# Windowed attention with a fused feed-forward: how many tokens of Q and K lie in one partition, and how the block transposes are cut

## The chip, the cores and the metric

One core of one Trainium2 chip. The metric is the device time of one execution in microseconds (us). The kernel before took 408.87 us, the median of two runs (408.53 and 409.21).

## The reference, cut to what matters

```python
# q, k, v: [8 batches, 8 heads, 576 tokens, 64], float32; window 64, causal
scores = q @ k.T / 8;  mask = (0 <= i - j) & (i - j < 64)
attn   = softmax(where(mask, scores, -1e9)) @ v
x      = attn.transpose(0, 2, 1, 3).reshape(4608, 512)
out    = ((x @ w1) * (x @ w2)) @ w3 @ w_out          # w1, w2: 512x1024, w3: 1024x1024, w_out: 1024x512
```

## The kernel before, in words

The order of the work on every engine is written out by hand; each engine runs its own queue in that order. There are three strands.

**Attention, batch by batch.** `load_qk` (L199) brings Q or K of one batch into a tile `t16` of 128 partitions, cast from float32 to float16 on the way, by two DMAs of GpSimd (POOL), L203. Each DMA takes four of the eight heads (`hh` is the head's parity). A head lies in 32 partitions, and a partition holds TI = 18 consecutive tokens of 64 values: one run of 4,608 bytes in DRAM and 2,304 bytes in the tile. `transposes` (L206) then has VectorE (DVE) transpose 32x32 blocks, one instruction for K or Q and one head parity (L211): it reads 32 values of one token at a time, and what it writes along a row of `kT` or `qT` are the tokens of 32 partitions, which lie 18 positions (36 bytes) apart. Four such instructions make one batch. The tiles `t16`, `kT` and `qT` have two buffers each. `load_v` (L217, L223) loads V by DMAs of POOL, a block of 128 tokens of all heads at a time (rows of 64 values: 256 bytes in DRAM, 128 in the tile).

`scores(n)` (L235, matmul L249) makes the scores of a third of a batch in two PSUM tiles `a_ps` (both buffers of that pool); `weigh` takes their exponential on ScalarE (ACT, L259) and masks it with two `affine_select` on POOL (L267, L269). `values(d)` (a half of that third) multiplies with V (matmuls L296 for the first two batches, L312 after), again into `a_ps`; ACT forms the reciprocal of the sums by Ln and Exp (L302, L303 or L318 to L320), and DVE multiplies it in and writes `xT` (L304, or L321 and L322).

**The feed-forward**, nine groups of 512 tokens. `ffn_ab` (matmul L374, 8 for one of eight feature blocks) makes a and b in PSUM tiles `f_ps` (four buffers), ACT copies a out (L379), DVE multiplies (L380). `ffn_o` (matmul L392) multiplies with the product of w3 and w_out; DVE copies the result out (L394) and the SP queue stores it.

**The fold** of w3 with w_out, at the start: eight steps of transposes on TensorE (PE, L430), a DVE copy (L432), matmuls (L438) and a copy (L439). The weights come by DMAs of POOL (L413, L417, L423).

Order: K and Q of batch 0 are loaded first, then w_out and half of w3, then V and the rest; four transposes; the scores of batch 0 between fold steps; K and Q of batch 1; the values of batch 0; then `ffn_ab` of group 0 with the four transposes of batch 1 and the scores of batch 1; then the values of batch 1 with the four transposes of batch 2; then a loop over twelve ticks for a batch (`tick`, L342 on) in which the feed-forward of groups 1 to 8 is laid between. In a tick `scores` comes at every fourth, `values` at the next two. The list `late` says what else: K of the batch two ahead is loaded in tick 0 of a batch, Q in tick 1; V of the next batch in ticks 2, 3 and 5; the transposes of the next batch stand in ticks 1, 3, 5 and 7. Every DMA that POOL issues reports on one of eight completion counters, handed out in turn, so each waits for the one eight places before it.

Of the kernel before, what the change touches and what calls it, by code (L numbers as in the profile page):

```python
# [144 lines left out]
def kernel(  # L145
# [11 lines left out]
    nc = tc.nc  # L157
    B, H, S, D = q.shape
# [4 lines left out]
    NJ = H // 2  # L163
    TI = 18
# [31 lines left out]

    t16s, kTs, qTs = {}, {}, {}

    def load_qk(b, which):  # L199
        src = k if which == "k" else q  # L200
        t = sb.tile([P, 2, TI * D], FP16, name=which + "16", bufs=2)
        for hh in range(2):
            nc.gpsimd.dma_start(out=t[:, hh], in_=src[b, hh:H:2].rearrange("j (p r) d -> j p (r d)", r=TI))  # L203
        t16s[which, b] = t

    def transposes(b, which, hh):  # L206

        dst = kTs if which == "k" else qTs
        if hh == 0:
            dst[b] = sb.tile([P, 2, 2, S], FP16, name=which + "T")  # L210
        nc.vector.transpose(dst[b][:, hh].rearrange("q c (p i) -> q i c p", i=TI), t16s[which, b][:, hh].rearrange(  # L211
            "p (i c e) -> p i c e", c=2, e=32))

    def v_heads(b):
        return v16s[b % 2].rearrange("p c j (a e) -> p c (j a) e", a=2)[:, :, :, 0:D]
# [118 lines left out]
    def event(b, kind, ahead, *a):  # L334
        if b + ahead >= B:
            return
        do = {"load": load_qk, "t": transposes, "v": load_v, "copy": copy_v}[kind]
        do(b + ahead, *a)
# [102 lines left out]
    rows = 2 * 3 * B  # L441
# [32 lines left out]
    def fold_step(fc):  # L474
        if fc + 1 < 8:
            w3Ts[fc + 1] = fold_t(fc + 1)
        fold_mm(fc, w3Ts.pop(fc), act_cp if fc % 4 == 3 else dve_cp)

    load_qk(0, "k")
    load_qk(0, "q")  # L480
    load_wo()
    load_w3(0)
# [3 lines left out]
    for hh in range(2):  # L486
        transposes(0, "k", hh)
        transposes(0, "q", hh)
# [140 lines left out]
```

## Time and profile before

| | us |
|---|---|
| median of the two runs | 408.87 |
| the profiled execution, its own time | 407.49 |
| its span in the profile | 405.8 |

The profiled execution is one further run; its time is 1.69 us longer than the span that the profile covers. Busy time of an engine is summed over its instructions. PEclk is the clock granted to TensorE as a share of its full 2.4 GHz; 0.50 is its lower level, 1.2 GHz. The DMA column is the mean busy share of 16 DMA engines (over 1 where packets overlap).

### The profile page before, as it was taken

What the parts mean: (1) busy time and instruction counts of PE and PEld (TensorE: products, weight loads), DVE (VectorE), ACT (ScalarE), POOL (GpSimd) and SP (SyncE); (2) the same over time, 40 slices, a digit from 0 to 9 for tenths busy, and PEclk for the clock granted to TensorE, in tenths of its full rate; (3) what the DMA queues carried; (4) which work ended last, traced back from release to release, by engine and by line L of the source; (5) the groups of instructions that cost most, each with busy time, mean ns of one, the idle gap of its engine ahead of it and who ended that gap; (6) DMA issues with size and microseconds to landing.
All of it is one profiled execution on the core that took longest, in us unless ns stands there. A gap on an engine that the chain in (4) does not pass through costs nothing.

```text
span 405.8 us, 6273 instructions
## 1 busy us (share of the span) xinstructions
PE 291.7 (72%) x2474; PEld 153.8 (38%) x2474; DVE 300.1 (74%) x267; ACT 149.7 (37%) x256; POOL 169.0 (42%) x218
## 2 busy tenths in 40 slices
PE   8008895747067454987679567978696779999995
PEld 8006452223033212443234233855342335455442
DVE  2892756976956399779977997598969896655542
ACT  1003162125023602364426433524464337764220
POOL 6307943118046852186127704535424533540300
PEclk9757999569668855996889887989899789999999
DMA  5990499911409990129312980299206410020203
GB/s 61 203 188 17 40 165 160 144 15 32 48 28 104 121 128 0 54 69 138 22 52 62 133 38 27 80 124 52 80 28 39 46 55 29 26 80 1 106 1 107
DMA packets 64097, 29.47 MB, mean 73 GB/s; under 512 B 51088, under 2 KB 54416, under 8 KB 64064
## 3 DMA queue, kind: packets, MB, share of 16 engines
q0 software_dynamic: 58640, 19.45, 51.3%
q1 hardware_dynamic: 5280, 9.46, 6.6%
q8 instruction: 20, 0.33, 0.4%
q14 instruction: 13, 0.11, 0.1%
q10 hardware_dynamic: 144, 0.13, 0.1%
HBM read 38.80 MB, written 9.44 MB: 119 GB/s over the span
## 4 chain that ended last, share of the span: by engine, by line
PE 40%; DVE 26%; issue 16%; DMA 10%; POOL 6%; ACT 1%; DVEq 0%; POOLq 0%
PE f_ps L374 22%; PE f_ps L392 11%; DVE qT L211 10%; DVE kT L211 9%; DMA k<-in_k_dram 7%; PE a_ps L312 4%; DMA q<-in_q_dram 3%; DVE ab L380 3%; PE a_ps L249 2%; POOL pt L269 2%; POOL pt L267 2%; DVE xT L322 2%; DVE xT L321 1%; DVE t2k L394 1%; POOL v L223 1%
## 5 line engine op out<-in xcount | busy, mean ns | idle before, releaser
L374 PE MATMUL f_ps<-xT,w_sb 128*128 128x512 f16 (+1 forms) x640 | 151.5, 392 | 30.1 <-DVE ab L380 23.8
L267 POOL TENSOR_SCALAR_AFFINE_SELECT pt<-pt 128x512 f16<-128x512 f16 (+1 forms) x64 | 52.0, 813 | 169.8 <-ACT pt L259 169.8
L374 PEld LDWEIGHTS <-w_sb 128*128 128x128 f16 x640 | 64.3, 104 | 99.3 <-issue 52.4
L211 DVE STREAM_TRANSPOSE kT<-k 128x1152 f16<-128x1152 f16 x16 | 81.9, 5119 | 16.4 <-DMA k<-in_k_dram 16.1
L259 ACT ACTIVATE pt<-a_ps 128x1024 f16<-128x1024 f32 (+1 forms) x48 | 43.1, 950 | 118.3 <-PE a_ps L249 118.3
L211 DVE STREAM_TRANSPOSE qT<-q 128x1152 f16<-128x1152 f16 x16 | 82.1, 5134 | 0.1
L392 PE MATMUL f_ps<-wc_sb,ab 128*128 128x512 f16 (+1 forms) x296 | 75.9, 411 | 7.6 <-DVE ab L380 7.6
L380 DVE TENSOR_TENSOR ab<-f_ps,a_sb 128x512 f16<-128x512 f32 x72 | 51.4, 723 | 32.9 <-PE f_ps L374 18.4
L379 ACT COPY a_sb<-f_ps 128x512 f32<-128x512 f32 x72 | 41.8, 581 | 62.6 <-PE f_ps L374 62.6
L249 PE MATMUL a_ps<-qT,kT 32*128 32x128 f16 (+1 forms) x768 | 19.2, 234 | 63.2 <-DVE xT L322 29.0
L269 POOL TENSOR_SCALAR_AFFINE_SELECT pt<-pt 128x512 f16<-128x512 f16 (+1 forms) x64 | 51.9, 811 | 4.4
L392 PEld LDWEIGHTS <-ab 128*128 128x128 f16 x296 | 29.7, 105 | 44.3 <-issue 10.3
L223 POOL DMA_DIRECT2D v<-in_v_dram x40 | 34.1, 856 | 19.5 <-DMA k<-in_k_dram 17.4
L249 PEld LDWEIGHTS <-kT 32*128 32x128 f16 x768 | 13.7, 103 | 74.4 <-issue 44.2
L394 DVE COPY t2k<-f_ps 128x512 f32<-128x512 f32 (+1 forms) x36 | 24.8, 693 | 13.1 <-PE f_ps L392 12.4
L321 DVE TENSOR_TENSOR xT<-a_ps,r 64x384 f16<-64x384 f32 x36 | 19.6, 546 | 19.0 <-ACT r L320 19.0
L318 ACT ACTIVATE ln_s<-a_ps 64x384 f32<-64x384 f32 x36 | 17.5, 487 | 40.1 <-PE a_ps L312 40.0
L312 PEld LDWEIGHTS <-v 128*128 128x128 f16 x288 | 20.4, 106 | 9.2 <-issue 3.2
L312 PE MATMUL a_ps<-pt,v 128*128 128x128 f16 (+1 forms) x288 | 23.0, 229 | 0.0
L322 DVE TENSOR_TENSOR xT<-a_ps,r 64x384 f16<-64x384 f32 x36 | 20.2, 561 | 0.5
L320 ACT ACTIVATE r<-ln_s 128x384 f32<-128x384 f32 x36 | 18.8, 523 | 1.1
L319 ACT ACTIVATE ln_s<-a_ps 64x384 f32<-64x384 f32 x36 | 17.4, 482 | 0.4
(41 smaller groups left out, 147.5 us busy)
## 6 DMA issues: line engine op xcount, KB each, us to landing
out_dram<-t2k SPq DMA_DIRECT2D x35, 256.0 KB
k<-in_k_dram POOLq DMA_DIRECT2D x16, 288.0 KB, 11.4
q<-in_q_dram POOLq DMA_DIRECT2D x16, 288.0 KB, 12.1
v<-in_v_dram POOLq DMA_DIRECT2D x32, 128.0 KB, 11.1
w_sb<-in_moe_w_dram POOLq DMA_DIRECT2D x4, 512.0 KB, 12.2
ab<-in_moe_w_out_dram POOLq DMA_DIRECT2D x1, 1024.0 KB, 15.7
ab<-in_moe_w_dram POOLq DMA_DIRECT2D x2, 512.0 KB, 18.2
xT<-in_moe_w_dram POOLq DMA_DIRECT2D x2, 512.0 KB, 14.7
```

The lines of the kernel that those rows point to most:

```text
L211: nc.vector.transpose(dst[b][:, hh].rearrange("q c (p i) -> q i c p", i=TI), t16s[which, b][:, hh].rearrange("p (i c e) -> p i c e", c=2, ...
L223: nc.gpsimd.dma_start(out=vh[lo:P, c], in_=v[b, :, s0:s0 + P - lo, :].rearrange("h s d -> s h d"))
L249: nc.tensor.matmul(s_ps[j // 2][:, j % 2, o0:o0 + m], kT[part, a, c, k0:k0 + P], qT[part, a, c, q0:q0 + m], start=(c == 0), stop=(c == 1), ...
L259: nc.scalar.activation(pt[:, :, :, 0:w], s_ps, AF.Exp, bias=-SHIFT, scale=scale)
L267: nc.gpsimd.affine_select(out=sl, in_=sl, pattern=pat, compare_op=ALU.is_ge, fill=0.0, base=off, channel_multiplier=-1)
L269: nc.gpsimd.affine_select(out=sl, in_=sl, pattern=[[-s, m] for s, m in pat], compare_op=ALU.is_ge, fill=0.0, base=63 - off, channel_multip ...
L312: nc.tensor.matmul(o_ps[:, jj, o0:o0 + n], v16[:, si * 2 + bi, j0 + jj, a * D:a * D + P], pt[:, jj, a, c0:c0 + n], start=first, stop=(bi = ...
L374: nc.tensor.matmul(d[:, f * n + c0:f * n + c1], w[:, dc, (fc + f) * P:(fc + f + 1) * P], xT[:, dc, xc:xc + c1 - c0], start=first, stop=(dc ...
L379: act_cp(a_sb[:, 0:nf * n], a_ps[:, 0:nf * n])
L380: nc.vector.tensor_tensor(ab[:, fc:fc + nf, lo:hi], b_ps[:, 0:nf * n].rearrange("p (f n) -> p f n", f=nf), a_sb[:, 0:nf * n].rearrange("p ...
L392: nc.tensor.matmul(o_ps[:, 0:c1 - c0], ab[:, fc, t * P:t * P + P], wc_sb[:, fc, c0:c1], start=(fc == 0), stop=(fc == 7))
L394: cp(o_sb[:, c0:c1], o_ps[:, 0:c1 - c0])
```

## The change

A partition now holds two consecutive tokens (r = 2) of each of nine runs: head token 64 i + 2 p + r' is in partition p, run i. The DMAs are cut by pairs of heads (`j`), four for a load in place of two, each to 32 partitions; a run is 512 bytes in DRAM and 256 in the tile, 18 for each partition and DMA. The transposes are issued for each half `c` of the head dimension (32 of the 64 values), so two instructions of 576 elements a partition stand where one of 1152 stood; the tokens that one writes along a row lie two positions (4 bytes) apart. Tiles, buffers, matmuls and the order of the calls stay as they are.

```diff
+    def run(b):
+
+        return 2
+
     def load_qk(b, which):
         src = k if which == "k" else q
+        r = run(b)
         t = sb.tile([P, 2, TI * D], FP16, name=which + "16", bufs=2)
-        for hh in range(2):
-            nc.gpsimd.dma_start(out=t[:, hh], in_=src[b, hh:H:2].rearrange("j (p r) d -> j p (r d)", r=TI))
+        for j in range(NJ):
+            nc.gpsimd.dma_start(
+                out=t[32 * j:32 * j + 32].rearrange("p hh (i n) -> p (hh i) n", n=r * D),
+                in_=src[b, 2 * j:2 * j + 2].rearrange("hh (i p r) d -> p (hh i) (r d)", p=32, r=r))
         t16s[which, b] = t
 
     def transposes(b, which, hh):
 
         dst = kTs if which == "k" else qTs
+        r = run(b)
         if hh == 0:
             dst[b] = sb.tile([P, 2, 2, S], FP16, name=which + "T")
-        nc.vector.transpose(dst[b][:, hh].rearrange("q c (p i) -> q i c p", i=TI), t16s[which, b][:, hh].rearrange(
-            "p (i c e) -> p i c e", c=2, e=32))
+        rows = t16s[which, b][:, hh].rearrange("p (i r d) -> p i r d", r=r, d=D)
+        for c in range(2):
+            nc.vector.transpose(dst[b][:, hh, c].rearrange("q (i p r) -> q i r p", p=32, r=r),
+                                rows[:, :, :, 32 * c:32 * c + 32])
```

## Rows read from the trace of the kernel before

**Rows 1.** The page's busy times, and the chain that ended last by engine.

```profile
PE 291.7 (72%) x2474; PEld 153.8 (38%) x2474; DVE 300.1 (74%) x267; ACT 149.7 (37%) x256; POOL 169.0 (42%) x218
PE 40%; DVE 26%; issue 16%; DMA 10%; POOL 6%; ACT 1%; DVEq 0%; POOLq 0%
```

**Rows 2.** The page's groups of instructions: the transposes, and two DVE groups beside them.

```profile
L211 DVE STREAM_TRANSPOSE kT<-k 128x1152 f16<-128x1152 f16 x16 | 81.9, 5119 | 16.4 <-DMA k<-in_k_dram 16.1
L211 DVE STREAM_TRANSPOSE qT<-q 128x1152 f16<-128x1152 f16 x16 | 82.1, 5134 | 0.1
L380 DVE TENSOR_TENSOR ab<-f_ps,a_sb 128x512 f16<-128x512 f32 x72 | 51.4, 723 | 32.9 <-PE f_ps L374 18.4
...
L432 DVE COPY t2k<-f_ps 128x1024 f16<-128x1024 f16 x8 | 5.3, 675 | 6.1 <-PE f_ps L430 6.1
```

**Rows 3.** Busy time by stage: stretch, length, engines, PEclk, DMA share, GB/s.

```profile
59.50:125.00 65.50, 33.86 (x290) 15.12 (x289) 50.78 (x29) 17.03 (x29) 23.30 (x30) 0.77 0.74 73
125.00:340.00 215.00, 160.56 (x1280) 82.06 (x1279) 178.75 (x160) 91.31 (x158) 97.45 (x124) 0.84 0.61 69
340.00:395.00 55.00, 55.00 (x393) 27.02 (x393) 30.22 (x49) 28.36 (x50) 16.40 (x19) 1.00 0.11 40
```

**Rows 4.** The same stretches, L211 alone: DVE busy (count), PEclk, DMA share, GB/s.

```profile
59.50:125.00 65.50, 40.75 (x8) 0.77 0.74 73
125.00:340.00 215.00, 102.39 (x20) 0.84 0.61 69
```

**Rows 5.** Timeline of DVE, then of PE, around 200 us: start, length, instruction.

```profile
192.66 5.12 DVE L211 STREAM_TRANSPOSE kT<-k 128x1152 f16<-128x1152 f16 x1
...
198.97 0.56 DVE L322 TENSOR_TENSOR xT<-a_ps,r 64x384 f16<-64x384 f32 x1
...
199.58 0.64 PE L249 MATMUL a_ps<-qT,kT 32*128 32x128 f16 x30 [3.64 <-DVE xT L322]
200.16 3.17 PE L392 MATMUL f_ps<-wc_sb,ab 128*128 128x512 f16 x7
```

**Rows 6.** The chain in order of time: start, length, what.

```profile
1.61 9.65 DMA k<-in_k_dram
11.29 5.10 DVE kT L211
...
26.23 4.93 DVE qT L211
...
304.15 0.46 PE a_ps L312 x8
...
348.48 0.56 PE a_ps L249 x32
...
379.90 12.09 PE f_ps L374 x56
```

**Rows 7.** Timeline of POOL, its DMA issues at the start and at 41 us.

```profile
1.61 1.63 POOL L203 DMA_DIRECT2D k<-in_k_dram  x2 [0.15 <-issue]
...
11.55 0.88 POOL L223 DMA_DIRECT2D v<-in_v_dram  x1 [3.76 <-DMA k<-in_k_dram]
...
41.45 1.59 POOL L223 DMA_DIRECT2D v<-in_v_dram  x2
```

**Rows 8.** Three stretches of one microsecond: PEclk, DMA share and GB/s end the line.

```profile
6.00:7.00 1.00, 1.00 (x22) 1.00 (x20) 0.00 (x0) 0.00 (x0) 1.00 (x3) 1.00 0.95 106
17.00:18.00 1.00, 0.00 (x0) 0.00 (x0) 1.00 (x1) 0.00 (x0) 0.87 (x2) 0.50 1.23 213
44.00:45.00 1.00, 1.00 (x5) 0.44 (x6) 1.00 (x2) 0.00 (x0) 0.93 (x2) 1.00 1.83 117
```

**Rows 9.** PE's matmuls from 125 to 340 us, shapes apart.

```profile
L374 PE MATMUL f_ps<-xT,w_sb 128*128 128x512 f16 x288 | 79.8, 428 | 16.2 <-DVE ab L380 11.1 <-DVE xT L304 2.7 <-DVE t2k L394 2.4
L392 PE MATMUL f_ps<-wc_sb,ab 128*128 128x512 f16 x160 | 45.4, 440 | 7.6 <-DVE ab L380 7.6
L374 PE MATMUL f_ps<-xT,w_sb 128*128 128x256 f16 x128 | 16.4, 288 | 4.3 <-DVE ab L380 4.3
```

## The prediction

> **What bounds the kernel now.** I began with the page's busy times and the chain by engine [rows 1]. PE and DVE are about equally busy (72% and 74%), and both stand in the chain, so an average does not say which of them binds. The groups [rows 2] show what DVE does: 32 transposes of 5.1 us are 164 of its 300 us, where its other instructions take 0.7 us. Per element a transpose takes 5119 / 1152 = 4.44 ns, the L380 row 723 / 512 = 1.41 ns, the L432 copy 675 / 1024 = 0.66 ns.
>
> Then the stages [rows 3, 4]. From 340 to 395 us no transpose is left and everything else goes on: there PE is busy all 55 us and its granted clock is 1.00 (2.4 GHz), DVE is at 30 of 55. From 125 to 340 us 20 transposes take 102 us of DVE, PE is busy 161 of 215 us, and the clock is 0.84. From 59.5 to 125 us eight take 41 of 65.5 us, PE is at half. The timeline [rows 5] shows how: a transpose runs from 192.66 to 197.78, the multiplications that free `a_ps` stand behind it and end at 199.53, and PE, whose next scores need that buffer, waits 3.64 us. Behind the gap the clock is at its lower level: seven matmuls take 3.17 us, 0.45 each, against 12.09 / 56 = 0.216 in the packed stretch [rows 6]. So DVE binds by what queues behind a long instruction, and each gap is paid again in slow matmuls. At the start it binds outright: the first K lands at 1.61 + 9.65 = 11.3, four transposes run back to back to 26.23 + 4.93 = 31.2, and only then does PE get its first scores [rows 6].
>
> **The change, part by part.** *Transposes.* 32 instructions of 1152 elements become 64 of 576. No row shows one of the new shape. Upper bound: the same 4.44 ns an element, 2.56 us each, no gain. Lower bound: the fastest DVE row above, 0.66 ns an element, 0.38 us. I take the rate of the L380 row, 1.41 ns: 0.8 us. My reason is that no other DVE row is near 4.44 ns, and what is peculiar to this one is that it writes each element 36 bytes from the last; with 4 bytes four neighbours lie within 16. So 64 x 0.8 = 51 us in place of 164: 113 us less DVE.
>
> The Trainium skill (SBUF — State Buffer, the note on cachelines under Door 1) says that accesses are at full rate if at least two fall into the same 16-byte line, and that each step to another line costs. The 4.44 ns at a 36-byte step [rows 2] agree with its penalty. Its full rate at the 0.96 GHz of the VectorE page would be an estimate of 0.6 us plus a start for 576 elements, and some 9 us less DVE than I take.
>
> *DMA issues.* Two DMAs a load become four. A POOL issue takes about 0.8 us, whether for 128 rows or for 512 to 1024 (1.63 and 1.59 us for two) [rows 7]. I take 0.8: 32 x 0.8 = 25 us more on POOL, 194 of it in all. This lies beside PE and DVE. In the loop POOL can have K's, Q's and three of V's issues in one piece between two masks: 11 x 0.8 = 9 us, now 7 x 0.8 = 5.6; the masks queued behind them are needed a third of a batch later, about 10 us, so it fits, with little to spare. Upper bound: the issue costs in proportion to rows, 0.8 / 128 x 576 = 3.6 us.
>
> *DMA transfer.* A load moves the same 576 KB, in pieces of 256 bytes. The rate is bounded by three stretches [rows 8]: V's pieces of 128 bytes ran at 117 GB/s, the loads as they are at 106 in the first stretch, rows of the weights at up to 213. That is 2.8 to 5.6 us for a load.
>
> The Trainium skill (DMA: Bandwidth & Descriptors, Specifications) speaks against this part: pieces under 512 bytes do not reach line rate. V's 117 beside 213 GB/s agree; by that rule alone a load would be near the 5 us end.
>
> *Waits.* POOL's ninth DMA waits for its first: V's issue at 11.55 stood 3.76 us until K had landed [rows 7]. Thirteen DMAs a batch in place of nine make that nearer: V's first issue in a batch now waits for K's first of the same batch, issued 8 x 0.8 = 6.4 us before. Landing within that costs nothing; masks are queued behind on POOL, and PE's values wait for masks.
>
> **The sum**, made against the profiled execution (407.49 us; span 405.8, so 1.7 outside).
>
> To 31.2 us: K and Q of batch 0 are 1.18 MB. Eight issues end at 1.6 + 6.4 = 8.0, so Q lands between 9.5 and, at 106 GB/s if data moves from 3 us on, 14.1. I take 12. DVE has K's first half done by then, six transposes remain: 12 + 6 x 0.8 = 16.8 in place of 31.2, so 14.4 less (12 to 19).
>
> 31.2 to 59.5: folds, masks and first values, PE mostly busy; unchanged, 28.3. The weights it needs must come 14 us sooner; at 213 GB/s [rows 8] all 4.7 MB issued first are in by about 28, and the late ones are not needed until some 35.
>
> 59.5 to 125: DVE is the queue. Eight transposes go from 5.1 to 1.6: 28 us less, 65.5 - 28 = 37.5. PE needs 96 x 0.216 = 21 us for the feed-forward here, plus a few for attention, so it does not bind before that.
>
> 125 to 340: PE becomes the bound. At the full clock, counts from [rows 9] and prices from [rows 6]: 448 x 0.216 + 128 x 0.108 + 28 values x 0.46 + 15 scores x 0.56 = 97 + 14 + 13 + 8 = 132 us. DVE needs 178.8 - 102.4 + 20 x 1.6 = 108 us, 82% of that, so some waits of under a microsecond stay; after gaps that short I expect no drop of the clock. I take PE at 91%, 145 us, plus 5 us where the loop starts and loads of two batches crowd POOL: 150. That is 65 less. Bounds: 97% and nothing, 136; 80% and 5, 170.
>
> 340 to the end: 65.8, no transposes, unchanged.
>
> Span: 16.8 + 28.3 + 37.5 + 150 + 65.8 = 298.4; with the 1.7 outside, 300. The median of the runs before lies 1.4 above the profiled execution, so 302.
>
> **The rivals.** (a) *The loads hold POOL up.* A quarter of a load lands later than the 6.4 us after its issue, V's issue waits, the masks behind it come late and PE idles into its lower clock. For: POOL already waited so [rows 7], and the pieces are small. Against: a quarter is 144 KB, little over 1 us at 117 GB/s. Price: if it lands after 11 us, 5 us for POOL and some 3 of slow matmuls in each of five loop batches: 302 + 40 = 342.
>
> (b) *Transposes only halved in price per element*, 1.6 us an instruction rather than 0.8. For: nothing in the trace has this shape. Then DVE needs 108 + 32 = 140 in the loop, above PE's 132; the loop takes about 165, the stage before 12 more, the start 5 more: 334.
>
> (c) *The transpose's rate belongs to the operation, not to its step.* 64 x 2.56 is the same 164 us, queued behind in halves. Against: 4.44 ns is over three times any row beside it. The start gains 1 to 2 us, the rest stands: about 405, no difference.
>
> (d) *Slower: POOL becomes the engine that binds*, because an issue costs by its rows, 3.6 us. Then 64 x 3.6 = 230 us replace 26 and POOL has 373. In the loop POOL is now busy 97 us for five batches [rows 3], 19.5 each; without 3.2 and with 8 x 3.6 = 29 it needs 45, where a batch takes 215 / 5 = 43: 10 us more in all. Q of the first batch is issued by 30 and its transposes end some 7 us later than now, and the loads of batches 1 to 3 cost PE perhaps 5: 407 + 22, about 430. It decides from 3 us an issue on. Against: V's 512 to 1024 rows in 0.8 us [rows 7].
>
> **How the numbers follow.** The forecast (about 283 to 322 by its own bounds) has 0.64, (a) 0.18, (b) 0.10, (c) 0.04, (d) 0.04. For the range I go from 280 (97% in the loop, cheap transposes, nothing lost at its start) up to 345, which takes in (a) and (b) and leaves out (c), (d) and worse mixtures. A measurement of this kernel tells about 2% from no change. Faster by over 2%: 0.64 + 0.18 + 0.10 = 0.92; within 2%: 0.04; slower: 0.04.
>
> **What would show it.** Right: L211 as 64 instructions of about 0.8 us and some 50 us in all; first scores at about 17 us; PE's waits for L322 and L380 nearly gone; granted clock near 1.00 in the loop; the loop's last waits on PE itself; L203 as 64 issues of about 0.8 us. Wrong: 2.5 us for L211 (c), issues over 2 us (d), or POOL waiting for K's or Q's DMA in every batch with PE waiting for masks at L269 (a). If DVE is cheap and PE is still idle, the stretch from 59.5 us on, with its short queues of feed-forward work, is where I would have been too hopeful.

## The result, and the profile after

The changed kernel takes 297.61 us (two runs, 297.04 and 298.18) where the kernel before took 408.87: a ratio of 0.7261, 95% interval 0.7212 to 0.7311. The prediction was 302, with 280 to 345. The profiled execution took 298.18 us, its span is 296.5. In the new file the transposes are line 221 (211 before), the loads of K and Q line 208 (203), and what stands behind them is ten lines further down (L259 for L249, L384 for L374, L402 for L392, L332 for L322, L279 for L269).

First the page of the changed kernel, busy times and the chain by engine, as in [rows 1].

```profile
PE 264.2 (89%) x2474; PEld 145.7 (49%) x2474; DVE 189.2 (64%) x299; ACT 149.9 (51%) x256; POOL 189.5 (64%) x250
...
PE 50%; POOL 16%; DMA 13%; DVE 11%; issue 5%; ACT 2%; DVEq 0%; POOLq 0%
```

DVE lost 111 us and POOL gained 20. PE does the same 2,474 matmuls but is busy 27 us less, because far fewer run at the lower clock (the mean granted clock is 0.97, where it was 0.85). DVE fell from 26% of the chain to 11%; what grew there is POOL, from 6% to 16%.

The groups, as in [rows 2]:

```profile
L390 DVE TENSOR_TENSOR ab<-f_ps,a_sb 128x512 f16<-128x512 f32 x72 | 48.9, 684 | 31.9 <-ACT a_sb L389 15.7
...
L221 DVE STREAM_TRANSPOSE kT<-k 128x576 f16<-128x576 f16 x32 | 23.9, 794 | 8.0 <-DMA k<-in_k_dram 7.7
...
L221 DVE STREAM_TRANSPOSE qT<-q 128x576 f16<-128x576 f16 x32 | 23.7, 791 | 3.4 <-DMA q<-in_q_dram 3.3
L208 POOL DMA_DIRECT2D k<-in_k_dram x32 | 21.5, 678 | 5.8 <-DMA w_sb<-in_moe_w_dram 4.0
```

A transpose of half the size takes 0.79 us, not half of 5.12; all 64 are busy 47.6 us where the 32 were busy 164. (The mean of one is a little above busy time by count, since neighbours overlap.) An issue on POOL takes 0.68 us with its 576 pieces.

The stages, as in [rows 3] (same columns), between the same events as before: the first matmul of the first `ffn_ab`, the first matmul of the loop (125.06 before, 80.58 now), and the first scores behind all transposes (340.05 before, 230.41 now).

```profile
44.90:80.60 35.70, 27.08 (x291) 13.26 (x290) 22.70 (x37) 16.15 (x27) 24.20 (x32) 1.00 1.41 122
80.60:230.50 149.90, 138.71 (x1284) 74.92 (x1282) 109.94 (x179) 92.38 (x160) 113.06 (x148) 0.98 0.92 100
230.50:285.50 55.00, 55.00 (x392) 27.07 (x391) 30.55 (x49) 28.38 (x50) 16.43 (x19) 1.00 0.11 40
```

65.5 us became 35.7, and 215 became 149.9; the stretch without transposes is as it was. In the loop PE is now busy 139 of 150 us and its granted clock is 0.98 (0.84 before). The same stretches for L221 alone, as in [rows 4]:

```profile
44.90:80.60 35.70, 11.83 (x16) 1.00 1.41 122
80.60:230.50 149.90, 29.93 (x40) 0.98 0.92 100
```

The chain's beginning, one piece of the stage of batch 1 and one of its end, as in [rows 6]:

```profile
6.52 5.82 DMA q<-in_q_dram
12.46 1.48 DVE qT L221 x2
13.94 1.33 DVE kT L221 x2
15.27 1.34 DVE qT L221 x2
...
47.78 13.07 DMA v<-in_v_dram
...
270.41 12.09 PE f_ps L384 x56
```

Q lands at 12.3 us, and the last transpose of batch 0 is done at 16.6, where it was 31.2. From the 56 packed matmuls on (379.90 before, 270.41 after, 109.5 us earlier) the two executions are alike. So the 109 us are: 14.5 by the first scores, 30 in the stage of batch 1, 65 in the loop. In the stage of batch 1 the chain no longer runs through transposes for the most part: from 44.3 to 68.5 us it is V's DMA and POOL's issues and masks.

### The profile page after: what moved, and what is told of

The parts are those of the page before. It is cut to its first block, busy times and chain, and to the rows that moved or that the text cites. A ratio compares the mean times of both kernels' runs of the same rounds, so it can differ in the third digit from the quotient of the medians.

```text
span 296.5 us, 6359 instructions
## 1 busy us (share of the span) xinstructions
PE 264.2 (89%) x2474; PEld 145.7 (49%) x2474; DVE 189.2 (64%) x299; ACT 149.9 (51%) x256; POOL 189.5 (64%) x250
## 4 chain that ended last, share of the span: by engine, by line
PE 50%; POOL 16%; DMA 13%; DVE 11%; issue 5%; ACT 2%; DVEq 0%; POOLq 0%
PE f_ps L384 26%; PE f_ps L402 17%; DMA v<-in_v_dram 7%; DMA k<-in_k_dram 5%; PE a_ps L322 4%; POOL pt L279 4%; POOL pt L277 4%; DVE kT L221 3%; PE a_ps L259 3%; POOL v L233 3%; POOL k L208 2%; DVE ab L390 2%; DVE qT L221 2%; DMA q<-in_q_dram 2%; DVE xT L332 2%
## 5 line engine op out<-in xcount | busy, mean ns | idle before, releaser
L384 PE MATMUL f_ps<-xT,w_sb 128*128 128x512 f16 (+1 forms) x640 | 133.3, 361 | 2.5 <-DVE xT L314 2.4
L384 PEld LDWEIGHTS <-w_sb 128*128 128x128 f16 x640 | 60.4, 98 | 59.3 <-issue 5.6
L269 ACT ACTIVATE pt<-a_ps 128x1024 f16<-128x1024 f32 (+1 forms) x48 | 43.1, 950 | 61.6 <-PE a_ps L259 61.6
L402 PE MATMUL f_ps<-wc_sb,ab 128*128 128x512 f16 (+1 forms) x296 | 68.6, 381 | 3.1 <-DVE ab L390 3.1
L390 DVE TENSOR_TENSOR ab<-f_ps,a_sb 128x512 f16<-128x512 f32 x72 | 48.9, 684 | 31.9 <-ACT a_sb L389 15.7
L279 POOL TENSOR_SCALAR_AFFINE_SELECT pt<-pt 128x512 f16<-128x512 f16 (+1 forms) x64 | 52.1, 814 | 4.4
L402 PEld LDWEIGHTS <-ab 128*128 128x128 f16 x296 | 28.0, 99 | 35.0 <-DVE ab L390 5.3
L221 DVE STREAM_TRANSPOSE kT<-k 128x576 f16<-128x576 f16 x32 | 23.9, 794 | 8.0 <-DMA k<-in_k_dram 7.7
L259 PE MATMUL a_ps<-qT,kT 32*128 32x128 f16 (+1 forms) x768 | 17.9, 219 | 11.3 <-DVE xT L332 5.1
L221 DVE STREAM_TRANSPOSE qT<-q 128x576 f16<-128x576 f16 x32 | 23.7, 791 | 3.4 <-DMA q<-in_q_dram 3.3
L208 POOL DMA_DIRECT2D k<-in_k_dram x32 | 21.5, 678 | 5.8 <-DMA w_sb<-in_moe_w_dram 4.0
L328 ACT ACTIVATE ln_s<-a_ps 64x384 f32<-64x384 f32 x36 | 17.6, 488 | 14.9 <-PE a_ps L322 14.5
L208 POOL DMA_DIRECT2D q<-in_q_dram x32 | 21.0, 663 | 5.5 <-DMA v<-in_v_dram 2.9
L259 PEld LDWEIGHTS <-kT 32*128 32x128 f16 x768 | 12.5, 96 | 22.0 <-issue 16.9
L322 PEld LDWEIGHTS <-v 128*128 128x128 f16 x288 | 18.2, 98 | 8.8 <-issue 1.7
L322 PE MATMUL a_ps<-pt,v 128*128 128x128 f16 (+1 forms) x288 | 20.9, 215 | 1.5 <-POOL pt L279 1.5
L332 DVE TENSOR_TENSOR xT<-a_ps,r 64x384 f16<-64x384 f32 x36 | 20.2, 561 | 0.5
```

The costliest lines, as they stand in the source:

```text
L208: nc.gpsimd.dma_start(out=t[32 * j:32 * j + 32].rearrange("p hh (i n) -> p (hh i) n", n=r * D), in_=src[b, 2 * j:2 * j + 2].rearrange("hh ...
L221: nc.vector.transpose(dst[b][:, hh, c].rearrange("q (i p r) -> q i r p", p=32, r=r), rows[:, :, :, 32 * c:32 * c + 32])
L259: nc.tensor.matmul(s_ps[j // 2][:, j % 2, o0:o0 + m], kT[part, a, c, k0:k0 + P], qT[part, a, c, q0:q0 + m], start=(c == 0), stop=(c == 1), ...
L269: nc.scalar.activation(pt[:, :, :, 0:w], s_ps, AF.Exp, bias=-SHIFT, scale=scale)
L279: nc.gpsimd.affine_select(out=sl, in_=sl, pattern=[[-s, m] for s, m in pat], compare_op=ALU.is_ge, fill=0.0, base=63 - off, channel_multip ...
L322: nc.tensor.matmul(o_ps[:, jj, o0:o0 + n], v16[:, si * 2 + bi, j0 + jj, a * D:a * D + P], pt[:, jj, a, c0:c0 + n], start=first, stop=(bi = ...
```

## The experiments

What was to be told apart: is the price of a transpose a matter of where it writes (the step between neighbouring elements), of its halved shape, or did the gain come from loads that land sooner? And what binds now?

**Only the cut into halves**, on the kernel before:

```diff
-        nc.vector.transpose(dst[b][:, hh].rearrange("q c (p i) -> q i c p", i=TI), ...
+        rows = t16s[which, b][:, hh].rearrange("p (i d) -> p i d", d=D)
+        for c in range(2):
+            nc.vector.transpose(dst[b][:, hh, c].rearrange("q (p i) -> q i p", i=TI),
+                                rows[:, :, 32 * c:32 * c + 32])
```

> The loads of before (18 tokens a partition, two DMAs), and only the cut of each transpose into halves of the head dimension. Theory (the price of a transpose is its 36-byte write step): 64 instructions of about 2.56 us, 164 us of DVE in all, time 400 to 412, no gain. Rival 1 (the halved shape is what is cheap): about 0.8 us each, 51 us in all, time near 300. Rival 2 (the gain came from the loads that land sooner): 2.56 us and no gain here, as the theory; the next run tells these two apart.

Measured: 407.02 us, beside 406.98 for the kernel before in the same series (one run each). The group of K's transposes in its profile:

```profile
L213 DVE STREAM_TRANSPOSE kT<-k 128x576 f16<-128x576 f16 x32 | 82.0, 2741 | 13.5 <-DMA k<-in_k_dram 13.2
```

Twice the instructions at half the busy time of one (82.0 / 32 = 2.56 us), nothing gained. The shape is not the cause; rival 1 falls.

**The changed kernel with 18, 9, 6, 3 and 1 tokens a partition.** Only one number differs:

```diff
     def run(b):
-        return 2
+        return 18
```

> The changed kernel with 18 tokens a partition: four DMAs a load by pairs of heads, halved transposes, but the write step is 36 bytes again and the pieces of a load are 4,608 bytes. Theory: 2.56 us a transpose, first scores at about 29 us (loads land earlier than before, eight halves of 2.56 follow), time 390 to 410. Rival 1: 0.8 us, near 300. Rival 2 (loads): 2.56 us a transpose, but time under 360, since the waits for K and Q are gone.

> Nine tokens a partition: write step 18 bytes, pieces of 2,304 bytes. Theory in its strict form (full price as soon as no two neighbours lie within 16 bytes): 2.5 us a transpose and 390 to 410, as with 18. If instead the price grows evenly with the step: about 1.6 us and 325 to 345.

> Six tokens a partition: write step 12 bytes, so that four elements take three lines of 16 bytes; pieces of 1,536 bytes. Strict theory: three of four elements open a new line, about 2.0 to 2.2 us a transpose, 360 to 385. Even growth with the step: about 1.3 us, 310 to 325. If 12 bytes are still cheap (0.8 us): 290 to 298, no slower than the changed kernel, as the loads have fewer pieces.

> Three tokens a partition: write step 6 bytes, pieces of 768 bytes (a third fewer than with two). If the price goes by elements for each 16-byte line and two or more are free (6 bytes: 2.7 in a line), 0.8 us a transpose and 290 to 298, as the changed kernel or a little under it by faster loads. If every new line costs something: 1.0 to 1.1 us, 300 to 310.

> One token a partition: write step 2 bytes, pieces of 256 bytes in DRAM, twice as many as with two. The transposes' price stays at 0.8 us if 4 bytes were already free; what grows is the loads. If pieces do not matter as long as the loads are ahead: 297 to 300. If the number of pieces decides when K and Q land (rival a of the prediction): landing over 8 us, POOL waiting for K and Q, 303 to 320.

The changed kernel itself was timed once more beside the last two:

> The changed kernel once more, timed beside the others on one chip: 296 to 299.

The group of K's transposes in each profile, with 18, 9, 6, 3 and 1 tokens:

```profile
L221 DVE STREAM_TRANSPOSE kT<-k 128x576 f16<-128x576 f16 x32 | 82.0, 2739 | 4.7 <-DMA k<-in_k_dram 4.4
```

```profile
L221 DVE STREAM_TRANSPOSE kT<-k 128x576 f16<-128x576 f16 x32 | 84.1, 2813 | 5.2 <-DMA k<-in_k_dram 4.9
```

```profile
L221 DVE STREAM_TRANSPOSE kT<-k 128x576 f16<-128x576 f16 x32 | 64.4, 2153 | 4.9 <-DMA k<-in_k_dram 4.6
```

```profile
L221 DVE STREAM_TRANSPOSE kT<-k 128x576 f16<-128x576 f16 x32 | 33.7, 1129 | 7.1 <-DMA k<-in_k_dram 6.9
```

```profile
L221 DVE STREAM_TRANSPOSE kT<-k 128x576 f16<-128x576 f16 x32 | 22.9, 754 | 9.3 <-DMA k<-in_k_dram 9.1
```

| tokens a partition | write step, bytes | one transpose, ns | time, us |
|---|---|---|---|
| 18 | 36 | 2739 | 396.03 (one run) |
| 9 | 18 | 2813 | 403.12 (one run) |
| 6 | 12 | 2153 | 364.12 (one run) |
| 3 | 6 | 1129 | 305.41 (four runs) |
| 2 | 4 | 796 | 297.62 (four runs) |
| 1 | 2 | 754 | 302.11 (one run) |

The shape is the same in all six, and the price runs with the step up to somewhere between 12 and 18 bytes, then it is flat. It is what a charge for each new line of 16 bytes gives: the straight line through 6 and 12 bytes reaches the flat price (2739 to 2813 ns) at 15.4 to 15.9 bytes. By that reading, step s opens 576 x s / 16 lines: 432 at 12 bytes, 216 at 6, 144 at 4. From 12 to 6 bytes that is (2153 - 1129) / 216 = 4.7 ns a line; with it and a fixed 0.12 us, 4 bytes come to 0.80 us (measured 0.80) and a line for each of the 576 elements to 2.83 (measured 2.74 and 2.81). At 2 bytes the lines alone would give 0.46 us, measured is 0.75: there another floor holds, about 1.1 ns an element. So even growth without end (the alternative for 9 tokens) falls, and so does the thought that two or more elements in a line make it free: with 2.7 in a line a transpose still costs 1.4 times that with four.

In time, 3 tokens are slower than 2: ratios to the kernel before of 0.7453 (0.7395 to 0.7511) and 0.7285 (0.7234 to 0.7336) in one series. With 1 token, transposes are a little cheaper and the time 4.5 us longer. Its K and Q come in twice as many pieces, and the waits of DVE for them grew from 11.0 us (7.7 and 3.3 in the groups of the changed kernel) to 15.2; landing itself was not over 8 us in the median (4.7 us for K, 7.1 for Q), as the expectation's second case wanted. What the expectation left out is the issue: with 1,152 pieces it takes 0.81 us in place of 0.66, POOL is busy 199 us in place of 189, and its share of the chain is 24%, where the two profiles of the changed kernel have 16% and 11%. So the 4.5 us fit both the dearer issues and the later loads; the two were not told apart. One run alone, but outside the 296.4 to 298.9 of the changed kernel's four in that series.

*The loads by themselves.* The kernel with 18 tokens differs from the one that is only cut into halves by its four DMAs a load, and transposes cost the same: 396.03 against 407.02, 11 us less. The groups show 8.8 of them: DVE waited 13.2 us for K's DMAs there and 4.4 here. Between the events named above, 2.3 us of the gain lie ahead of the first `ffn_ab`, 5.6 in the stage of batch 1 and 3.9 in the loop; 0.8 are lost behind it. These are single runs, and the kernel with 9 tokens, whose loads are cut likewise and whose transposes take 4 us more in all, gained only 4 us. So rival 2 holds for at most about a tenth of the 109 us; the rest, 396 to 297.6, came with the step. That second part has the loads' pieces grow smaller as well. The step is the layout that the load makes, so the smaller pieces come with it; two DMAs a load with the new step were not tried.

**Every transpose twice:**

```diff
         for c in range(2):
-            nc.vector.transpose(...
+            for _ in range(2):
+                nc.vector.transpose(...
```

> The changed kernel with every transpose issued twice (the same values written again): 128 of 0.8 us, 51 us more on DVE, which is then at about 240 us. If PE binds the loop and DVE has room: under 10 us more, 300 to 308, nearly all of it at the start. By the prediction's working, where DVE with 1.6 us for a transpose needs more than PE in the loop: 320 to 335.

Measured: 342.92 us (one run), above both ranges. The two stages in its profile (51.4 and 99.9 are the first `ffn_ab` and the first of the loop):

```profile
51.40:99.90 48.50, 31.31 (x293) 14.72 (x289) 34.80 (x53) 16.93 (x29) 25.73 (x34) 0.82 1.07 91
99.90:275.80 175.90, 146.22 (x1280) 77.75 (x1279) 141.15 (x219) 91.53 (x159) 111.37 (x146) 0.92 0.80 85
```

Who waits for whom says what binds (line, the one waited for, us in total, times, the longest); the changed kernel's line for the same wait stands second, one line number lower:

```profile
PE a_ps L260 <- DVE xT L333: 16.4, 8, 4.0
```

```profile
PE a_ps L259 <- DVE xT L332: 5.1, 7, 2.4
```

52 us more on DVE cost 45: 6.5 at the start, 13 in the stage of batch 1, 26 in the loop. DVE is busy only 80% of the loop and yet it is the loop's brake, as PE's scores wait three times as long for the multiplication that stands behind the transposes, and PE's granted clock is 0.92. That PE binds the loop and DVE has room is thus true of the changed kernel only just: with 28% more work on DVE in the loop (141 us for 110) its queue is the limit again.

**Some transposes taken out:**

```diff
-        for c in range(2):
+        if b >= 2:
+            nc.vector.memset(dst[b][:, hh, 1], 0.0)
+        for c in range(2 if b < 2 else 1):
             nc.vector.transpose(...
```

> The changed kernel, but from batch 2 on the second half of the head dimension of K and Q is not transposed; a memset stands in its place, so half of each of those scores is left out. 24 transposes of 0.8 us become memsets of some 0.2 to 0.5 us, 8 to 14 us less on DVE, nothing else moves. If PE binds the loop (theory): 0 to 4 us less, 294 to 298. If DVE still decides at the 0.9 us a us that the doubled transposes showed: 286 to 290.

Measured: 294.09 us (one run). A memset took 0.30 us, and DVE was busy 180.6 us, 8.6 less than in the changed kernel; the time is 3.5 less. That is inside the first range, but only 2.3 under the lowest of the four runs above. So a microsecond taken off DVE is worth about 0.4 by this one run (3.5 / 8.6), where one added cost 0.87 (45 / 52) on the way to the doubled kernel. PE binds for the most part, not wholly.

**Where the loads of K and Q stand.** In the changed kernel's POOL timeline the eight issues of batch 2 stand one by one, most of them behind an earlier DMA that has to land, and the masks of `scores(3)` behind them; then comes K of batch 3, whose transposes follow closely:

```profile
51.84 0.67 POOL L208 DMA_DIRECT2D k<-in_k_dram  x1 [2.07 <-DMA w_sb<-in_moe_w_dram]
54.40 0.66 POOL L208 DMA_DIRECT2D k<-in_k_dram  x1 [1.90 <-DMA w_sb<-in_moe_w_dram]
...
61.13 0.66 POOL L208 DMA_DIRECT2D q<-in_q_dram  x1 [1.00 <-DMA v<-in_v_dram]
61.80 0.66 POOL L277 TENSOR_SCALAR_AFFINE_SELECT pt<-pt 128x512 f16<-128x512 f16 x1
...
82.18 2.71 POOL L208 DMA_DIRECT2D k<-in_k_dram  x4
```

The timeline of DVE and PE of the same execution at the loop's start:

```profile
90.39 1.50 DVE L221 STREAM_TRANSPOSE kT<-k 128x576 f16<-128x576 f16 x2 [3.27 <-DMA k<-in_k_dram]
...
106.64 1.05 DVE L237 COPY v<-v 64x512 f16<-64x512 f16 x1 [4.75 <-DMA v<-in_v_dram]
```

```profile
99.35 0.86 PE L259 MATMUL a_ps<-qT,kT 32*128 32x128 f16 x30 [2.44 <-DVE xT L332]
```

And the loop of the changed kernel in two parts, its first 36 us and the rest:

```profile
80.60:116.70 36.10, 29.00 (x229) 13.06 (x228) 21.21 (x35) 16.65 (x28) 29.21 (x40) 0.91 1.20 115
116.70:230.50 113.80, 109.72 (x1059) 61.87 (x1058) 88.73 (x144) 75.73 (x132) 83.84 (x108) 1.00 0.84 95
```

After 116.7 us PE is busy 96% at the full granted clock, idle for 4.1 of 113.8 us; in the 36.1 us before it is idle for 7.1, at a clock of 0.91. Most of what the loop still loses, it loses there. Three kernels move loads:

```diff
     transposes(1, "k", 1)
-    load_qk(2, "q")
     ffn_ab(0, 3)
...
     scores(3)
+    load_qk(2, "q")
```

> The changed kernel with Q of batch 2 issued behind scores(3), so that the masks of scores(3) no longer stand behind four issues that wait for DMAs. If that wait of POOL is on the path (rival a, what is left of it): 2 to 4 us less, 293 to 296. If not, or if Q then lands late for its transposes: 297 to 300.

```diff
         values(d)
+        if d == 7:
+            load_qk(3, "k")
         if d == 9:
...
     load_v(2, 4, 5)
-    load_qk(3, "k")
```

> The changed kernel with K of batch 3 issued behind values(7), before scores(5), where POOL is idle, in place of after V of batch 2. If the start of the loop waits for that K (the chain has 6.0 us of its DMA): 3 to 6 us less, 291 to 295. If the masks of scores(5) are held up by as much: 297 to 300.

> Both moves of loads. If each takes a wait of its own off the path: 289 to 293. If the first only moves the wait to the second: as the better of the two.

Measured, as ratios to the kernel before: Q later 0.7334 (0.7287 to 0.7382), 299.01 us; K of batch 3 earlier 0.7192 (0.7146 to 0.7238), 293.33 us; both 0.7246 (0.7185 to 0.7306), 296.69 us. The first did not help. The waits of DVE for Q's DMA in its profile are 5.7 us in three places, 3.3 in two before: the wait was moved, not removed. The second did. In its profile the issues lie at 71.50, and the first transposes of batch 3 no longer wait:

```profile
71.50 2.64 POOL L208 DMA_DIRECT2D k<-in_k_dram  x4
74.47 1.10 POOL L277 TENSOR_SCALAR_AFFINE_SELECT pt<-pt 128x1024 f16<-128x1024 f16 x1 [0.33 <-ACT pt L269]
...
88.16 1.50 DVE L221 STREAM_TRANSPOSE kT<-k 128x576 f16<-128x576 f16 x2
```

Its four runs took 292.9 to 293.8, the changed kernel's four 296.4 to 298.9 in another series: some 4 us less. The profiles put it at the loop's start: from the loop's first matmul to the scores that come at 116.7 us in the changed kernel takes 30.5 us (81.71 to 112.24) in place of 36.1, though it begins 1.1 us later. It is the fastest version that was run. Both moves together (five runs, 295.6 to 300.6) are no better than the second alone. What is left at that place is a wait for V: in the changed kernel DVE's copy of V waits 4.75 us for V's DMA (the line at 106.64 above), in the fastest kernel still 4.43, with the multiplications for PE queued behind it. No run moved V.

## Why the prediction was right

*What bound the kernel.* The reading that DVE binds through what queues behind 5 us transposes, and that each gap is paid again in matmuls at the lower clock, held: with short transposes most of PE's waits in the loop went, the granted clock rose from 0.84 to 0.98, and in the doubled kernel both came back in part.

*The price of a transpose* was the one number that no row of before had. It was taken as 0.8 us from the rate of the L380 row, between 0.38 and 2.56, because the step of the writes was what set L211 apart. It measured 0.79. The reason held as well, and this was more than the one result could say: the halves alone leave 2.56 us, and the price follows the step over six layouts. That the rate of another instruction, L380, gave the size is luck: no run ties the two, and the lines opened at 4 bytes give the 0.80 us by themselves. The Trainium skill's note on cachelines (SBUF — State Buffer, Door 1) names lines of 16 bytes, which agrees with the curve; that two accesses to a line are enough for full rate does not, by 1129 ns at 2.7 elements a line against 796 at four.

*The sum, stage by stage.* First scores: 16.8 forecast, 16.7 measured, with Q landing at 12.3 for 12. Folds: 28.3 and 28.2. Stage of batch 1: 37.5 and 35.7. Loop: 150 and 149.9, of which PE is busy 139 for the 132 of work that the matmuls need at full clock. Tail: 65.8 and 66.0. That the loop came out to the microsecond is partly luck, for its two allowances erred in opposite directions. PE was taken at 91% and was at 96% after 116.7 us; and the 5 us set aside for "loads of two batches crowd POOL" at the loop's start were real but too few, as moving one load alone made that part 5.6 us shorter.

*POOL and its waits.* 25 us more were forecast, 20 measured: an issue takes 0.68 rather than 0.8 us. (The 1.63 us of [rows 7] hold the very first issue, 0.92 us; the median before was 0.67 to 0.72.) In the loop's steady part no wait of POOL for a DMA is left. Rival (a) exists only before the loop, where the timeline shows issue by issue behind earlier DMAs (51.84 to 61.13 us), and for 0.45 us at its first batch, at 87.31. Rivals (c) and (d) fell with 0.79 us a transpose and 0.68 us an issue.

*Where the working was off.* Rival (b) put a transpose of 1.6 us at 334, with the loop at 165; the doubled kernel, which puts the same work on DVE, took 343, with the loop at 176. The step that failed there is the rate at which DVE can be filled: 140 us of DVE work were forecast to fit into 165, and 141 took 176. And what the loads bring by themselves was counted only at the start; the single run with slow transposes shows 5.6 us in the stage of batch 1 and 3.9 in the loop, the one with 9 tokens none in the loop (212.3 us, beside 212.1 with the old loads).

## What to carry to other kernels

Where an engine writes a transposed block, look at the distance between neighbouring elements on the writing side before the instruction count: here 36 bytes cost 3.5 times as much as 4, and a different split of tokens over partitions in the load moved it. Take the smallest step whose loads still arrive in time: 4 bytes beat both 6 (dearer transposes) and 2 (more pieces, dearer issues). And when a long instruction on an engine of 74% is cut short, price the stages by what the next engine needs at full clock, then look at the first batch, where the loads that used to be hidden come to the surface.

## What the runs showed of the hardware that was not expected

The price of a transpose is nearly a straight line in its write step: 4.7 ns for each new 16 bytes, from 4 to 12 bytes, flat at 2.7 to 2.8 us from 18 on, with a floor of 0.75 us at 2 bytes. Four elements to a line (0.80 us) are within 6% of that floor; a threshold at two had been thought possible.

A load of four DMAs, each to 32 partitions in 512-byte pieces, was no slower to land than the two of 4,608-byte rows: the medians from issue to landing on the page are 5.3 us (K) and 6.4 us (Q) for 144 KB where they were 11.4 and 12.1 for 288 KB, and the first K was in at 8.7 us in place of 11.3. With the same four DMAs the size of the pieces mattered little: 5.1 and 5.9 us with 4,608 bytes in DRAM, 4.7 and 7.1 with 256. The issue on POOL follows the number of pieces only slowly: the median is 0.54 us with 64 of them, 0.66 with 576 and 0.81 with 1,152.

An engine that is busy 80% of a stage can be its brake: in the doubled kernel 31 us more on DVE made the loop 26 us longer, although DVE stood idle for 35 us of it.
